# The last token tile for the first expert taken on chip, more second products held back, and the first search of the router split in two

## The chip, the cores and the metric

One core of one Trainium2 chip runs the whole program. Time is device time in microseconds (us). Five engines run side by side: TensorE (PE: products, with weight loads as PEld), VectorE (DVE), ScalarE (ACT), GpSimd (POOL) and SyncE (SP). Each works through its own instructions in order; semaphores tie them together. Sixteen DMA engines serve all queues; GpSimd starts the gathers and the accumulating copies itself, SyncE the loads of weights, ScalarE the stores of tokens.

## The reference

Three layers follow each other. The first is an attention with a decaying state. The second is a dense layer over 3072 tokens of 384 features with 2048 hidden ones. The third gives every token to one of 8 experts, each with exactly 384 places, in the order of the sorted logits:

```
x = attention(r, k, v, w, u)                 # 4 x 768 tokens -> (3072, 384)
h = x @ w_in                                 # (3072, 2048)
x = (h * sigmoid(1.702 * h)) @ w_out
logits = x @ w_gate                          # (3072, 8)
for idx in argsort(-logits.flatten()):       # greedy: token, expert = idx // 8, idx % 8
    if assigned[token] < 0 and counts[expert] < 384:
        assigned[token] = expert; counts[expert] += 1
out[mask_e] = relu(x[mask_e] @ w1[e]) @ w2[e]      # w1: 384 x 1024, w2: 1024 x 384
```

## The kernel before

Work is cut into 24 units of 128 tokens and 8 blocks of 3 units (384 tokens). Block by block the dense layer runs over 16 chunks of 128 hidden features: a first product (`Ffn.g1`, line 1207, 9 instructions: 3 feature groups by 3 pairings of high and low halves of the operands), the activation on ScalarE with the low half on VectorE, and a second product (`Ffn.g2` or single parts of it, line 1235, 9 instructions) into three accumulators, one for each tile of 128 tokens. The experts use the same class with 8 chunks each.

The program writes all instructions out by hand order. A small planner (`Issue`, object `sc`) keeps an estimated time and, for each engine, an estimated moment at which it is free. Chains of work are Python generators with a rank. They give durations to the planner, and while the loop emits PE products the planner lets chains go on whose time has come. `sc.until(...)` emits filler products until a condition holds in the plan. What the plan has put down is the order on each engine; what waits at run time is settled by semaphores.

Around the change the order is this. In the last block, the first products of all 16 chunks come first, each with a thin product for the logits (line 1479). Second products of chunks 0 and 1 (`NIN = 2`) follow at once; those of chunks 2 to 13 (`NHOLD = 12`) are held as activated tiles in a ring named `hold`, 14 and 15 in the ordinary ring. After the loop the logits of the last block are put together (lines 1569 to 1578), and the router starts.

The router (`Router.route`) works for one expert after the other. `best` finds each token's best open expert and a sort key, and ends in a first comparison table; `search` finds in five steps the threshold that fills some expert with 384 tokens. Each step is a table on VectorE, 24 small counting products on PE (line 429), and a few short operations (lines 431 to 436). Then come ranks, and `slots` (line 460) turns ranks into row numbers `idx` with a one-hot table and 24 small products (line 492). `best` for the next expert is put between these steps. Meanwhile PE does the 42 held parts (`parts_left`), tile by tile, and at the end of each tile `store_x2` copies the accumulator (line 1350) and stores it to DRAM as rows of `x2d` (line 1353). When the parts are out, `spin_wide` emits fillers (line 1783).

For expert i, `gather` (line 1671) fetches 384 rows of `x2d` by three indirect DMAs on GpSimd (line 1684), turns them round with PE transposes (line 1700), and writes a high half on ScalarE (line 1709) and a low half on VectorE (line 1711). `weights` loads eight pieces of 384 KB through the `hold` ring; `split_weights` makes a high half on ScalarE (line 1640) and a low half either on VectorE (line 1648) or by a negated copy (line 1657) and an accumulating DMA from GpSimd (line 1665). Expert 0 starts when its `ffn` is there and its first piece of weights is split:

```
sc.until(lambda: "ffn" in EX[0] and ("raw1", 0, 0) in wdone)
```

Later experts start as soon as theirs are there; until then PE may do up to two chunks of second products of the expert before.

Of the kernel before, what the change touches and what calls it, by code (L numbers as in the profile page):

```python
# [167 lines left out]
class Router:  # L168
# [7 lines left out]
    def __init__(self, nc, S, pool, bank, NJ, E, cap):  # L176
        self.nc, self.S, self.pool, self.work, self.bank, self.busy = nc, S, pool, None, bank, False
        self.NJ, self.E, self.cap = NJ, E, cap
        self.L = pool.tile([128, NJ, E], F32, name="L")

    def consts(self):
# [14 lines left out]
        nc.gpsimd.iota(jp[:, :, 1], pattern=[[0, NJ]], base=0, channel_multiplier=1,  # L196
                       allow_small_or_imprecise_dtypes=True)
# [33 lines left out]

    def t(self, name, shape, dt=F32, bufs=2):
        return self.work.tile(shape, dt, name=name, bufs=bufs)
# [7 lines left out]
    def best(self):  # L241
# [3 lines left out]
        V, L, t = self.nc.vector, self.L, self.t  # L245
        m = t("m", [128, NJ])
        V.tensor_reduce(m, L, axis=AX.X, op=OP.max)
        yield
        eq = t("eq", [128, NJ, E])
        V.tensor_tensor(eq, L, m[:, :, None].to_broadcast([128, NJ, E]), op=OP.is_equal)  # L250
        yield
        V.tensor_tensor(eq, eq, self.W[:, None, :].to_broadcast([128, NJ, E]), op=OP.mult)
        key = t("key", [128, NJ], I32)
        bits = m.bitcast(I32)
        V.tensor_scalar(key, bits, 31, -2147483648, op0=OP.arith_shift_right, op1=OP.bitwise_or)
        yield
        self.wb = t("best", [128, NJ])
        V.tensor_reduce(self.wb, eq, axis=AX.X, op=OP.max)
        V.tensor_tensor(key, key, bits, op=OP.bitwise_xor)
        yield  # L260
        self.oh = t("oh", [128, NJ, E], BF)
        V.tensor_tensor(self.oh, eq, self.wb[:, :, None].to_broadcast([128, NJ, E]), op=OP.is_equal)
        yield

        self.key = key
        h0 = t("h0", [128, NJ], I32)
        V.tensor_scalar(h0, key, 33 - HALVES[0][0].bit_length(), None, op0=OP.logical_shift_right)
        yield
        c = t("c", [128, NJ, 2], BF)
        V.tensor_copy(c, h0[:, :, None].to_broadcast([128, NJ, 2]))  # L270
        self.G0 = []
        for _ in self.compare(self.G0, c, HALVES[0][0]):
            yield
# [14 lines left out]
    def digits(self):  # L288
# [4 lines left out]
        hl = t("hl", [128, sum(ns), NJ], I32)  # L293
# [10 lines left out]
        hf = t("hf", [128, sum(ns), NJ])  # L304
# [4 lines left out]
    def route(self, out, i, found, taken):  # L309
# [4 lines left out]
        if i == 0:  # L314
            for _ in self.best():
                pass
            yield (("V", 3.4),)
# [142 lines left out]
    def slots(self, out):  # L460
# [41 lines left out]
        out["idx"] = idx  # L502
        yield (("V", 0.5),)

@with_exitstack
def kernel(ctx, tc, r, k, v, w, rk, u, us, w_in, w_out, w_gate, w1, w2, out):
# [37 lines left out]
    NIN = 2  # L544
    DLAG = 1.5
    NPE = 9
    NHOLD = 12
# [20 lines left out]
    x2d = dr.tile([NT, Dm], F32, name="x2d")  # L568
# [627 lines left out]
    class Ffn:  # L1196
# [4 lines left out]
        def g1(self, f):  # L1201
# [3 lines left out]
            for kt in range(KT):  # L1205
                for n, (a, b_) in enumerate(((0, 0), (0, 1), (1, 0))):
                    T.matmul(p, self.l1(kt, f, a), (self.xh, self.xl)[b_][:, kt],  # L1207
                             start=(kt == 0 and n == 0), stop=(kt == KT - 1 and n == 2))
                    if kt == KT - 1 and n == 2:
                        self.g1_done(f)  # L1210
                        sc.add(self.act(self, f, p, lambda: R["g1"].free(i)), 0)
                    if fine[0]:
                        sc.tensor(0.1735)
                if not fine[0]:
# [102 lines left out]
    todo = [0, 0]  # L1317

# [20 lines left out]
    def store_x2(blk, tt, acc):  # L1339
# [13 lines left out]
        nc.scalar.dma_start(x2d[j * 128:(j + 1) * 128, :], x2)  # L1353
# [119 lines left out]

    def thin_logits(f, ps):
# [54 lines left out]
    for s in range(len(seq) + 2):  # L1529
        slot[0] = s  # L1530
        fine[0] = s < begin[2]
        if s == begin[3]:
            router.consts()
            P.memset(wogp[:, NFS * 2 * E:].bitcast(F32), 0.0)
# [340 lines left out]
```

## Time and profile before

| | |
|---|---|
| three runs | 822.89, 824.23, 826.66 us (median 824.23) |
| the profiled execution | 822.38 us, its span 820.4 us |
| granted clock of TensorE | 0.998 of full speed |
| busy, of the span | PE 803.3 us (98%), PEld 756.6 (92%), DVE 622.8 (76%), ACT 472.7 (58%), POOL 140.6 (17%) |
| DMA | 105.85 MB, mean 129 GB/s |

Times in rows are counted from the first instruction. Busy time of PE includes filler products, which keep it running while it has nothing to do (lines 732 and 1783). A group's arrow shows the written tile and what it is made from. In square brackets stands the idle time of the engine just before, and what ended it.

### The profile page before, as it was taken

To read this page: it belongs to the slowest core of one execution; us is meant where nothing else is said; L and a number is where in the kernel's file an instruction comes from. 1 tells how busy PE (TensorE), PEld (TensorE's weight loads), DVE (VectorE), ACT (ScalarE), POOL (GpSimd) and SP (SyncE) were. 2 spreads that over 40 slices of the span, in tenths; PEclk is the share of its full clock that TensorE was granted. 3 is DMA by queue.
4 is the path that set the end of the run, shared out by engine and by line. 5 is a ranking of instruction groups with operands and counts; after the bars stand their busy time and mean duration, and the time that the engine had idled before them with its cause. 6 is when DMAs were issued, how large, how long until landed. Compare 5 with 4: busy or idle time off the path is not lost.

```text
span 820.4 us, 17510 instructions
## 1 busy us (share of the span) xinstructions
PE 803.3 (98%) x6608; PEld 756.6 (92%) x6608; DVE 622.8 (76%) x1424; ACT 472.7 (58%) x1178; POOL 140.6 (17%) x188
## 2 busy tenths in 40 slices
PE   8999999999999999999999999999999999999995
PEld 7898999999999999999999999988898988989995
DVE  9977898879879888888879827478888887875310
ACT  5754653575676686686676644214556645576421
POOL 1001001001201101100102000003334443454211
PEclk9999999999999999999999999999999999999999
DMA  9833634412313313303313000028889899989400
GB/s 289 227 114 107 205 117 138 130 28 84 112 32 106 112 27 98 111 23 103 111 26 107 6 12 20 2 80 223 224 222 246 240 262 244 267 226 332 89 30 29
DMA packets 46068, 105.85 MB, mean 129 GB/s; under 512 B 7352, under 2 KB 13344, under 8 KB 45984
## 3 DMA queue, kind: packets, MB, share of 16 engines
q1 hardware_dynamic: 30816, 68.21, 26.5%
q0 software_dynamic: 10416, 29.50, 16.5%
q10 hardware_dynamic: 4752, 7.03, 2.4%
q8 instruction: 51, 0.84, 0.4%
q14 instruction: 33, 0.27, 0.1%
HBM read 73.60 MB, written 10.03 MB: 102 GB/s over the span
## 4 chain that ended last, share of the span: by engine, by line
PE 84%; issue 6%; DMA 5%; DVE 2%; POOL 1%; ACT 1%; SPq 0%; POOLq 0%; ACTq 0%; DVEq 0%
PE g L1207 33%; PE acc L1235 33%; PE s L1071 3%; PE s L1153 3%; PE s L429 2%; DMA cvb<-x2d,idx 2%; PE s L809 2%; PE s L1148 1%; DMA hold<-in_w 1%; DMA nat_v<-in_v 1%; PE s L1088 1%; PE s L1103 1%; PE acc L732 1%; PE s L1479 1%; POOL out L1743 1%
## 5 line engine op out<-in xcount | busy, mean ns | idle before, releaser
L1235 PE MATMUL acc<-wk,gh 128*128 128x384 f32 x1080 | 283.2, 340 | 0.1
L1235 PEld LDWEIGHTS acc<-wk,gh 128*128 128x128 f32 x1080 | 193.3, 188 | 1.6 <-issue 0.6
L1235 PE MATMUL acc<-wk,gl 128*128 128x384 f32 x540 | 181.9, 337 | 0.0
L1207 PE MATMUL g<-xha,wk 128*128 128x384 f32 x576 | 166.1, 340 | 0.0
L1207 PE MATMUL g<-xhb,wk 128*128 128x384 f32 x576 | 164.5, 339 | 0.0
L1282 ACT ACTIVATE cvb<-cvb 128x384 f32<-128x384 f32 x240 | 122.7, 517 | 8.4 <-DVE cvb L1293 7.9
L1253 ACT ACTIVATE g<-g 128x384 f32<-128x384 f32 x128 | 60.9, 476 | 101.1 <-PE g L1207 95.9
L1207 PEld LDWEIGHTS g<-xha,wk 128*128 128x128 f32 x576 | 105.4, 188 | 1.1 <-issue 0.3
L1207 PEld LDWEIGHTS g<-xhb,wk 128*128 128x128 f32 x576 | 105.1, 188 | 0.3
L1235 PEld LDWEIGHTS acc<-wk,gl 128*128 128x128 f32 x540 | 101.4, 188 | 0.0
L1207 PE MATMUL g<-xlb,wk 128*128 128x384 f32 x288 | 97.5, 339 | 0.0
L1207 PE MATMUL g<-xla,wk 128*128 128x384 f32 x288 | 97.2, 338 | 0.0
L1056 POOL TENSOR_SCALAR_AFFINE_SELECT At<-dg 128x512 f32<-128x512 f32 x38 | 35.0, 944 | 361.1 <-DVE dg L1049 273.5
L1259 DVE TENSOR_TENSOR gl<-g,gh 128x384 fp32r<-128x384 f32 x116 | 63.5, 548 | 29.1 <-ACT gh L1256 28.9
L1266 ACT ACTIVATE gh<-g 128x384 fp32r<-128x384 f32 x64 | 31.4, 491 | 88.8 <-PE g L1207 81.5
L1269 DVE SCALAR_TENSOR_TENSOR gl<-g,gh 128x384 fp32r<-128x384 f32 x64 | 35.3, 552 | 43.7 <-ACT gh L1266 43.6
L1293 DVE TENSOR_TENSOR cvb<-cva,raw 128x768 f32<-128x768 f32 x60 | 57.2, 963 | 8.5 <-ACT cva L1350 4.8
L1256 ACT ACTIVATE gh<-g 128x384 fp32r<-128x384 f32 x116 | 56.5, 487 | 6.5 <-ACT cva L1350 2.4
L1640 ACT ACTIVATE wk<-hold 128x768 fp32r<-128x768 f32 x64 | 52.9, 840 | 10.3 <-DMA hold<-in_w 10.3
L1665 POOL DMA_DIRECT2D wk<-hold x51 | 46.4, 1026 | 65.1 <-ACT wk L1657 51.9
L1207 PEld LDWEIGHTS g<-xlb,wk 128*128 128x128 f32 x288 | 54.1, 188 | 0.1
L1207 PEld LDWEIGHTS g<-xla,wk 128*128 128x128 f32 x288 | 54.1, 188 | 0.0
(282 smaller groups left out, 1264.4 us busy)
## 6 DMA issues: line engine op xcount, KB each, us to landing
hold<-in_w SPq DMA_DIRECT2D x64, 384.0 KB, 7.7
wk<-hold POOLq DMA_DIRECT2D x51, 384.0 KB, 7.6
nat_m<-in_rk SPq DMA_DIRECT2D x15, 384.0 KB, 3.1
nat_v<-in_v SPq DMA_DIRECT2D x22, 256.0 KB, 2.9
raw<-in_w_in SPq DMA_DIRECT2D x7, 768.0 KB, 4.4
raw<-in_w_out SPq DMA_DIRECT2D x7, 768.0 KB, 4.7
nat_w<-in_w SPq DMA_DIRECT2D x22, 226.2 KB, 2.9
nat_k<-in_k SPq DMA_DIRECT2D x22, 224.0 KB, 2.6
```

Source lines behind the costliest of these rows:

```text
L1056: P.affine_select(At[s], dg[:, s::2][:, :, None].to_broadcast([128, HP, C]), pattern=[[0, HP], [1, C]], compare_op=OP.is_equal, fill=0.0, ...
L1207: T.matmul(p, self.l1(kt, f, a), (self.xh, self.xl)[b_][:, kt], start=(kt == 0 and n == 0), stop=(kt == KT - 1 and n == 2))
L1235: T.matmul(self.acc[tt], gs[a][:, tt * C:(tt + 1) * C], self.r2(f, b_), start=(f in self.cuts and n == 0), stop=(end and n == 2))
L1253: A.activation(p, p, AF.Gelu_apprx_sigmoid)
L1256: A.activation(gh, p, AF.Copy)
L1259: V.tensor_tensor(gl, p, gh.bitcast(F32), op=OP.subtract)
L1266: A.activation(gh, p, AF.Relu)
L1269: V.scalar_tensor_tensor(gl, p, 0.0, gh.bitcast(F32), op0=OP.max, op1=OP.subtract)
L1282: A.activation(t_[:, n], t_[:, n], AF.Copy, accum_out=put[n])
L1293: V.tensor_tensor(t_, x[:, None, :].to_broadcast([128, 2, Dm]), wgB[e // 4][:, (e % 4) * Dm:(e % 4 + 2) * Dm].rearrange("p (a d) -> p a d" ...
L1640: A.activation(Whi[key], raw, AF.Copy)
L1665: P.dma_start(out=Wlo[key].bitcast(F32), in_=raw, accum_op=OP.add)
```

## The change

The last block holds the second products of all chunks: `NIN = 0` and `NHOLD = 13`, so that 48 parts are left after the loop. The router's constants and `best` for all 24 columns are made in a chain `ahead` while the last block's first products run; when the last logits are there, `best` runs again for the 4 columns of the last position only (`redo`), and the plan allows 1.5 in place of 3.4 for it. The three copies of last logits become one.

`x2d` gets 128 rows of zeros at its end. For expert 0 the last tile (number 23) is numbered 24 in the row tables, so that the gathers fetch zeros for tokens of that tile and need not wait for its store. In their place, the last tile's copy in SBUF is multiplied with a one-hot matrix (an iota on GpSimd, compared on VectorE with the tile's ranks) into the accumulators, and the gathered rows are added with a product by the identity in place of a transpose. Afterwards `all_rows` computes the true row numbers, for the scatter, and restores the tables.

In `split_weights` the first piece of all takes the VectorE way, pieces 1 to 3 never do. In `best` the two chains of operations are interleaved. For expert chunk 0 the nine instructions of the first product are ordered so that those which need only high halves of x come first.

```diff
@@ Router
+        nc.gpsimd.iota(jp[:, NJ - 1, 0:1], pattern=[[0, 1]], base=NJ, ...)
+    def ahead(self):
+        for _ in self.best():
+            self.S.busy["V"] = max(self.S.t, self.S.busy["V"]) + 0.42
+            yield from self.S.room("V", 0.3)
+        self.begun = True
+        yield 0.1
@@ best(self, cols=None): on the columns `cols` of tiles kept from the first call
         V.tensor_reduce(m, L, axis=AX.X, op=OP.max)
         yield
+        V.tensor_tensor(eq, L, m..., op=OP.is_equal)
         yield
         V.tensor_scalar(key, bits, 31, -2147483648, ...)
+        V.tensor_tensor(eq, eq, self.W..., op=OP.mult)
         yield
         V.tensor_tensor(key, key, bits, op=OP.bitwise_xor)
+        V.tensor_reduce(wb, eq, axis=AX.X, op=OP.max)
         yield
+        V.tensor_scalar(h0, key, 33 - HALVES[0][0].bit_length(), None, op0=OP.logical_shift_right)
+        V.tensor_tensor(oh, eq, wb..., op=OP.is_equal)
         yield
+        V.tensor_copy(c, h0...)
         yield
+        (all columns: compare as before; else one compare of the chosen columns for each of two tables)
@@ route
-            for _ in self.best():
+            for _ in self.best(self.redo):
                 pass
-            yield (("V", 3.4),)
+            yield (("V", 1.5),)
+    def all_rows(self, out):
+        V.tensor_tensor(d, self.tt[:, 0:3], self.tt[:, 1:4], op=OP.subtract)
+        V.tensor_scalar(far, d, 128.0 * NJ - 0.5, -128.0, op0=OP.is_ge, op1=OP.mult)
+        V.tensor_tensor(out["idx"], d, far, op=OP.add)
+        V.memset(self.JP[:, NJ - 1, 0:1], NJ - 1.0)
+        V.memset(self.R[:, NJ - 1, 0, 0:1], NJ - 1.0)
@@ constants and tokens
-    NIN = 2
+    NIN = 0
-    NHOLD = 12
+    NHOLD = 13
-    x2d = dr.tile([NT, Dm], F32, name="x2d")
+    x2d = dr.tile([NT + 128, Dm], F32, name="x2d")
@@ Ffn.g1
+            steps = [(kt, n) for kt in range(KT) for n in range(3)]
+            if f == 0 and self.nf == NF3:
+                steps.sort(key=lambda x: x[1])
@@ store_x2
+        if (blk, tt) == (NBLK - 1, NU - 1):
+            kept.append((x2, sc.t, st))
+            for other in sent:
+                tc.declare_no_dep(st.ins, other.ins, ...)
+        elif (blk, tt) == (NBLK - 1, NU - 2):
+            EX[0]["x2"] = sc.t + 4.0          # before: set after the last part
@@ the last block's loop
+    def no_rows():                             # zeros to the last tile's rows and the 128 rows behind
+        P.memset(t_, 0.0)
+        for rows in (x2d[NT - 128:NT, :], x2d[NT:, :]):
+            nc.scalar.dma_start(rows, t_)
+    def ahead():                               # waits for the logits of all blocks but the last
+        router.late_consts(...); router.Gt = [...]; P.memset(...) twice
+        router.redo = slice(NC - 1, None, NC)
+        yield (("P", 1.8),)
+        yield from router.ahead()
-    sc.until(lambda: todo[0] == 0)
+    sc.until(lambda: router.begun)
@@ split_weights
-        if sc.busy["D"] > sc.t + BEHIND:
+        if m == 0 or m > 3 and sc.busy["D"] > sc.t + BEHIND:
             while sc.t < ready:
                 yield 0.1
-            if sc.busy["V"] <= sc.t + 0.2 and sc.busy["D"] > sc.t + BEHIND:
+            if m == 0:
+                yield from sc.room("V", 0.2)
+            if m == 0 or sc.busy["V"] <= sc.t + 0.2 and sc.busy["D"] > sc.t + BEHIND:
                 order[0] += 1
                 V.tensor_tensor(Wlo[key], raw, Whi[key].bitcast(F32), op=OP.subtract)
@@ gather, for i == 0
+            near = pair_[:, 1]
+            P.iota(near, pattern=[[1, NB]], base=1, ...)
+            yield from sc.room("V", 0.4)
+            V.tensor_scalar(near, near, o["rs"][:, NJ - 1:NJ], None, op0=OP.is_equal)
+            while not kept or sc.t < kept[0][1] + 0.8:
+                yield 0.1
+            first = [psum.tile([128, 512], F32, name=f"acc{a}") for a in range(NU)]
+            for a in range(NU):
+                for kt in range(KT):
+                    T.matmul(first[a][:, kt * C:(kt + 1) * C], kept[0][0][:, kt * 128:(kt + 1) * 128],
+                             near[:, a * C:(a + 1) * C], start=kt == 0, stop=False, ...)
+                yield (("T", 0.7),)
@@ land, for i == 0
+                    T.matmul(ps[:, kt * C:(kt + 1) * C], xg[a][:, kt * 128:(kt + 1) * 128], ident,
+                             start=False, stop=True, ...)
+                sc.t += 0.64
@@ gather, after the three tiles have landed
+        if i == 0:
+            router.all_rows(o)
```

## Rows read from the trace of the kernel before

**Rows 1.** Busy time by stretch: us, engines' busy time, granted clock, DMA share, GB/s.

```profile
550.24:564.30 14.06, 13.84 (x148) 10.76 (x148) 11.14 (x46) 7.30 (x12) 6.10 (x7) 1.00 0.71 184
564.30:596.64 32.34, 31.35 (x306) 28.39 (x305) 26.50 (x103) 17.80 (x28) 9.31 (x11) 1.00 0.95 252
...
665.10:699.50 34.40, 32.55 (x308) 29.66 (x308) 27.76 (x115) 18.93 (x31) 12.62 (x17) 1.00 0.99 269
```

**Rows 2.** Chain of waits near 493 us: start, us, what (one second product).

```profile
492.75 1.56 PE acc L1235 x9
```

**Rows 3.** Timeline of PE: start us, us, engine, line, operation, idle before.

```profile
529.15 0.76 PE L429 MATMUL s<-oh,cvc 128*128 128x8 bf16 x24
...
550.24 1.33 PE L1783 MATMUL g<-xhb,wogp 128*128 128x512 f32 x5
...
559.86 0.76 PE L429 MATMUL s<-oh,cvc 128*128 128x8 bf16 x24
560.85 0.52 PE L1700 MATMUL s<-ident,cvb 128*128 128x128 f32 x3 [0.23 <-DMA cvb<-x2d,idx]
...
563.38 0.76 PE L429 MATMUL s<-oh,cvc 128*128 128x8 bf16 x24
...
564.32 0.34 PE L1207 MATMUL g<-xha,wk 128*128 128x384 f32 x1
```

**Rows 4.** Timeline of VectorE, same columns.

```profile
511.96 0.56 DVE L1259 TENSOR_TENSOR hold<-g,hold 128x384 fp32r<-128x384 f32 x1 [1.38 <-ACT hold L1256]
...
525.28 0.35 DVE L247 TENSOR_REDUCE m<-L 128x24 f32<-128x192 f32 x1
...
527.12 0.17 DVE L267 TENSOR_SCALAR h<-key 128x24 int32<-128x24 int32 x1
527.32 0.19 DVE L270 CAST c<-h 128x48 bf16<-128x48 int32 x1
527.62 1.03 DVE L284 TENSOR_TENSOR cvc<-c,raw 128x768 bf16<-128x768 bf16 x2
...
552.60 0.16 DVE L501 TENSOR_TENSOR idx<-r_tt 128x3 int32<-128x3 f32 x1
...
554.79 0.44 DVE L270 CAST c<-h 128x48 bf16<-128x48 int32 x1
...
556.21 0.35 DVE L384 TENSOR_TENSOR oh<-oh,r_keep 128x192 bf16<-128x192 bf16 x1
...
563.17 0.55 DVE L1711 TENSOR_TENSOR xla<-s,xha 128x384 fp32r<-128x384 f32 x1
```

**Rows 5.** Timeline of ScalarE's queue: stores of the last two tiles.

```profile
542.63 0.33 ACTq L1353 DMA_DIRECT2D x2d<-cva  x1
...
550.96 0.33 ACTq L1353 DMA_DIRECT2D x2d<-cva  x1
```

**Rows 6.** Timeline of GpSimd: first and third of expert 0's three gathers.

```profile
554.08 1.15 POOL L1684 DMA_INDIRECT cvb<-x2d,idx  x1 [49.04 <-DVE key L255]
...
556.97 0.95 POOL L1684 DMA_INDIRECT cvb<-x2d,idx  x1 [0.30 <-issue]
```

**Rows 7.** Groups of GpSimd: count, busy us, mean ns, idle before.

```profile
L184 POOL IOTA r_d<- 128x128 f32 x1 | 0.2, 233 | 0.0
```

**Rows 8.** Timeline of PE near 132 us: 8 float products, 16 instructions.

```profile
132.54 1.16 PE L1071 MATMUL s<-nat_r,nat_k 48*128 48x128 f32 x16
```

**Rows 9.** Timelines of VectorE, then PE, at the starts of experts 3 and 4.

```profile
664.35 0.55 DVE L1711 TENSOR_TENSOR xlb<-s,xhb 128x384 fp32r<-128x384 f32 x1
...
665.12 0.42 PE L1207 MATMUL g<-xhb,wk 128*128 128x384 f32 x1
...
693.98 0.55 PE L1700 MATMUL s<-ident,cvb 128*128 128x128 f32 x3 [1.80 <-DMA cvb<-x2d,idx]
```

**Rows 10.** Timeline of VectorE near 604 us: a low half of weights.

```profile
604.22 0.96 DVE L1648 TENSOR_TENSOR wk<-hold,wk 128x768 fp32r<-128x768 f32 x1 [0.44 <-ACT wk L1640]
```

**Rows 11.** DMA issues of the page: count, KB each, us from issue to landing.

```profile
wk<-hold POOLq DMA_DIRECT2D x51, 384.0 KB, 7.6
```

More of the change, by code (lines that the diff above doesn't have):

```diff
@@ L263, in best @@
         yield
[L265 to L267 removed]
+        V.tensor_copy(c, h0[:, :, None].to_broadcast([128, n, 2]))
+        self.key, self.wb, self.oh = self.tiles[2], self.tiles[3], self.tiles[4]
         yield
[L269 to L273, printed above, removed]
+        if n == NJ:
+            self.G0 = []
+            for _ in self.compare(self.G0, self.tiles[6], HALVES[0][0]):
+                yield
+        else:
+            step, half = cols.step, NJ // len(self.Gt)
+            w = HALVES[0][0]
+            for h, g in enumerate(self.Gt):
+                at = slice(h * half + cols.start, (h + 1) * half, step)
+                k = len(range(NJ)[at])
+                V.tensor_tensor(g[:, cols.start::step, :w].rearrange("p j (a b) -> p j a b", b=2),
+                                self.pairs(self.tiles[6][:, at], w), self.numbers(k, w), op=OP.is_ge)
+                yield
@@ L1317 @@
     todo = [0, 0]
+    kept, sent = [], []
+    EX = [dict() for _ in range(E)]
     rest, stored = {}, set()
@@ L1352, in store_x2 @@
         stored.add((blk, tt))
-        nc.scalar.dma_start(x2d[j * 128:(j + 1) * 128, :], x2)
+        st = nc.scalar.dma_start(x2d[j * 128:(j + 1) * 128, :], x2)
+        if (blk, tt) == (NBLK - 1, NU - 1):
+            assert j == NJ - 1
+            kept.append((x2, sc.t, st))
+            for other in sent:
+                tc.declare_no_dep(st.ins, other.ins, reason="the first expert's gathers leave out these rows")
+        elif (blk, tt) == (NBLK - 1, NU - 2):
+            EX[0]["x2"] = sc.t + 4.0
         if blk < NBLK - 1:
@@ L1472 @@
     parts_left = [(f, tt) for tt in range(NU) for f in range(NIN, NFS)]
+    def no_rows():
+        yield from wait("cva")
+        R["cva"].free(R["cva"].new())
+        t_ = cv.tile([128, Dm], F32, name="cva", bufs=NCVA)
+        P.memset(t_, 0.0)
+        for rows in (x2d[NT - 128:NT, :], x2d[NT:, :]):
+            nc.scalar.dma_start(rows, t_)
+        yield (("P", 0.5),)
+    def ahead():
+        while todo[0] or not late:
+            yield 0.2
+        router.late_consts(cv.tile([128, 128], BF, name="raw64", bufs=2))
+        router.Gt = [cv.tile([128, NJ // 2, 128], BF, name="cvc", bufs=NCVC) for _ in range(2)]
+        for g_ in router.Gt:
+            P.memset(g_.rearrange("p a b -> p (a b)").bitcast(F32), 0.0)
+        router.redo = slice(NC - 1, None, NC)
+        yield (("P", 1.8),)
+        yield from router.ahead()
     def thin_logits(f, ps):
@@ L1585 @@
         spin()
-    EX = [dict() for _ in range(E)]
     scat = []
@@ L1683, in gather @@
             xg.append(pair_[:, a % 2])
-            P.indirect_dma_start(out=xg[a], out_offset=None, in_=x2d,
-                                 in_offset=bass.IndirectOffsetOnAxis(ap=o["idx"][:, a:a + 1], axis=0))
+            g_ = P.indirect_dma_start(out=xg[a], out_offset=None, in_=x2d,
+                                      in_offset=bass.IndirectOffsetOnAxis(ap=rows[:, a:a + 1], axis=0))
+            if i == 0:
+                for x in kept:
+                    tc.declare_no_dep(g_.ins, x[2].ins, reason="the first expert's gathers leave out these rows")
+                sent.append(g_)
             sc.busy["D"] = max(sc.busy["D"], sc.after((("P", 1.04),))) + 0.6
```

105 lines of the change are left out of this document (64 added, 41 removed).

## The prediction

> **What bounds the kernel now.** I read the clock first, then busy time by stretch, then the timelines of TensorE (PE), VectorE (DVE), ScalarE (ACT) and GpSimd (POOL) from 490 to 700 us. The granted clock is 1.00 in every stretch, and PE is busy nearly all the time [rows 1]; the clock plays no part. But busy is not useful. From 550.24 to 564.32 us PE runs the filler product of line 1783, which nobody reads, between small products of the router [rows 3]. These 14.1 us, between the last second product of the dense layer and the first product of expert 0, are the only large hole, and the change works there.
>
> What ends the hole? The router's first search starts at 525.28 and ends in the row numbers `idx`, written by 552.76 [rows 4]. The first gather starts only at 554.08 [rows 6], 1.3 us later: it reads the stored tokens, and the store of the last tile is issued at 550.96 [rows 5]; 3.1 us lie between. So two chains end there almost together, with the store last. The third gather starts at 556.97; PE is released by its landing at 560.85 [rows 3, 6]. VectorE, held up by a step of the second search, writes the low half until 563.72 [rows 4], and the first product comes at 564.32.
>
> Behind the hole the stage is not free to move. Each expert needs its own search and gather. For expert 3 the low half ends at 664.90 and PE starts at 665.12; for expert 4 PE stands 1.80 us at a gather's transposes [rows 9]. The DMA share is 0.95 in expert 0's stretch and 0.99 in expert 3's, and VectorE is busy 26.5 of 32.3 us in the first [rows 1]. PE, the searches one behind the other, and the DMA run at almost the same pace there.
>
> **The change part by part.**
>
> *Second products held.* Chunks 0 and 1 of the last block lose their second product inside the loop. One takes 1.56 us [rows 2]; two, 3.12 us. PE does them later, as 6 more of the 42 parts that cover the search. So the search starts 3.12 us earlier and PE's total is unchanged. This holds if the two shorter slots stall nowhere: VectorE must do the same logits there, and from 508 on it sits idle 1.4 us of every 1.9 [rows 4]; I take 0 (bounds 0 and 1 us).
>
> *Search partly ahead.* The first step takes 525.28 to 528.65 for 24 columns [rows 4]. It is now done earlier for all, in that idle time, and again for 4 columns: 9 small operations and 2 compares. A dependent small operation follows its predecessor by 0.20 us (527.12 to 527.32). Six dependent steps make 1.2, three partners at half that 0.3, two small compares 0.3 to 0.4: 1.9 us for 3.4, so 1.5 saved. The first counting product waited until 529.15 [rows 3], 0.5 us longer, because the written plan put it there; the plan's allowance falls from 3.4 to 1.5, so it moves 1.9. I take 1.9 (bounds 1.4 and 2.2). With the 3.12 that is 5.0: `idx` at 547.75 instead of 552.76.
>
> *The gathers.* They leave out the last tile (zero rows stand in for it), so they wait for the store of the last but one, issued in the trace at 542.63 [rows 5]. With 3.12 earlier and 4 more parts of 0.52 before it, and its place among search steps, it stays near 541 to 542 and lands by 545. `idx` is last: gathers start near 547.9 instead of 554.08, 6.2 us earlier, and the third lands at 554.5 instead of 560.7.
>
> *The product from the chip.* One GpSimd iota of 384 columns (128 columns took 233 ns; I take 0.5, bounds 0.23 and 0.7 [rows 7]) stands in its queue behind the three gathers, so it ends near 552.3; one VectorE compare, 0.3; then 9 exact products of 128 columns. Such float products come as two instructions; 8 took 1.16 us [rows 8], so 9 take 1.3. The last tile's copy is ready near 551.4, since PE's parts now end near 550.9 (550.24, less 3.12, plus 3.12, plus 0.6 for the 24 small products of the slots, as long as a counting step of rows 3, that now fall before). So these end near 554.2, when the gather lands. The 9 products that replace 9 transposes cost 1.3 instead of 1.0 and lie mostly under the landing. The last three, ScalarE's copy of 0.5 and the plan's steps follow: expert 0 starts near 557.0 (bounds 555.6 by data alone, 558.5 with a VectorE collision as now). That is 7.3 us earlier. New order of the first chunk's products saves up to 0.5 inside these bounds.
>
> *First weights.* Their load follows the search, 5.0 us earlier; the second chunk's is no longer held to the end of the parts. The first low half is a VectorE subtract, 0.96 us [rows 10], instead of an accumulating DMA, which lands 7.6 us after issue [rows 11]. It arrives in time, but later splits wait in order behind it. Its queue place is where VectorE is planned free, which I put after the masking at 556.21 less 5.0 [rows 4]. The DMA stream as a whole starts 5 to 7 us earlier.
>
> *What is late next.* The second search. It moves 5.0 with `idx`, not 7.3, and gets new work on VectorE. The compare for the one-hot waits for an iota queued behind gathers that end 4.0 us after `idx` (554.08 to 557.92 for the three [rows 6], and 0.15 ahead), so 4.5 with the iota; the second search's instructions stand behind that wait. Placed after the masking (3.8 us behind `idx`), it costs 0.7 and the compare 0.3. The subtract costs 0.96, less a hole of 0.6 us while PE counts: 0.4. Restoring the row numbers, 5 small operations, costs 0.4. The second search now meets expert 0's first products 2 us sooner: 0.3. Sum 2.1. Interleaving the two halves of `best` hides a dependent step and a planned one, about 0.3 per search: 0.3 for expert 1, 1.2 by expert 4. So x of expert 1 comes 3.2 us earlier, of expert 4 4.1. Bounds: 0 if the wait stands right behind `idx` (4 us), 6 if all new work falls into holes.
>
> While PE is 7.3 early and x 3 to 4, second products fill for 1.56 each; by expert 3 both are used up already in the trace of before (PE starts it within 0.3 us of its x [rows 9]), so PE gets what the search gets: 4.1 us. From expert 5 on nothing more is lost. Sum: 7.3 less 3.2 given back = 4.1.
>
> On a lock: beside the first gather a cast of VectorE took 0.44 us, and ended with the gather, where the same cast took 0.19 in the first search [rows 4, 6]. The Trainium skill ("SBUF — State Buffer", Who interferes with whom) says that a cast or tensor_scalar in a two-port mode and a GpSimd instruction block each other for the whole instruction. By that rule all three gathers, now beside more of these operations, could each hold one for up to 1.1 us; by the row it is 0.25 once.
>
> **The rivals.**
>
> *PE keeps it all* (7.3 us): if the searches are not the limit behind the hole. For it: PE idles only 0.99 us in expert 0's stretch and 1.85 in expert 3's [rows 1]. Against: [rows 9]. Time 824.2 - 7.3 = 816.9.
>
> *The wait stands early, or gathers hold VectorE.* The one-hot's compare right behind `idx` makes VectorE wait 4.2 us instead of 0.7; or three holds of 1.1. The second search then moves 5.0 - 2.1 - 3.5, the interleaving gives back 1.2: 0.6 us, 823.6. For it: the queue is in order, and the row of 0.44 us. Against: the router's own steps are planned back to back there and take the place first. The lock rule above is one form of this.
>
> *The gathers still wait for the last store.* Parts end 0.6 later, so the first gather starts at 554.7 and nothing is gained: 824.8. Against: the dependence is declared away in both directions.
>
> *Slower: the first subtract finds no place.* All later splits of weights wait in order behind it. Its plan wants VectorE free within 0.2 us. If it slips three counting steps (3.5 us each, as 559.86 to 563.38 [rows 3]), it runs near 563, the next split's accumulate is issued near 566 and lands near 573, against a need at about 561: PE stands some 11.6 us after two first products, 4.3 more than the 7.3 won: 828.5. It decides from two slips on. For it: VectorE's load [rows 1]. Against: each counting step leaves a hole.
>
> **How the numbers follow.** The profiled execution took 822.38 us (span 820.4 and 2.0 around it); the median of the three runs is 824.23. 822.4 - 4.1 = 818.3 against the first, 820.1 against the median; I give 820.0. Chances: forecast 0.43 (own range 817.5 to 821.8, half of it below 820.1), PE keeps it all 0.22, early wait or lock 0.19, gathers still wait 0.07, slower 0.09. Half a per cent, 4.1 us, is about what a measurement of this kernel can tell from no change. Faster by more: 0.22 + 0.27 = 0.49; slower by more 0.09; between 0.42. The range reaches from 815.5 (all kept, by the data bound of 555.6) to 825.0, leaving out the slower case.
>
> **What would show it.** Right: the first masking step of the search about 5 us earlier; the first gather within 0.3 us of `idx` instead of 1.3; expert 0's first product near 557; fillers of line 1783 falling from 14 to about 6 us; and then the lead shrinking from 7 to about 4 by expert 3, with more fillers or standing ahead of experts 1 to 3. Wrong: a lead that stays at 7 through expert 4 (searches not the limit), a VectorE wait of 3 us right behind `idx`, a first gather later than 552, or a first split of weights after 558.

## The result: slower by 1.1%

The changed kernel takes 834.15 us (832.80 to 834.87, 4 runs), the kernel before 824.61 us beside it (822.89 to 826.66, 4 runs): ratio 1.0113, 95% interval 1.0086 to 1.0140. I forecast 820.0 and gave slower by more than half a per cent a chance of 0.09. The profiled execution took 834.09 us (span 832.4), so 12.0 us more span than before.

The same stretches after (us, engines' busy time, granted clock, DMA share, GB/s), against [rows 1]:

```profile
550.24:562.60 12.36, 11.26 (x112) 9.84 (x112) 8.12 (x31) 7.37 (x11) 5.03 (x8) 1.00 0.79 215
562.60:595.52 32.92, 32.77 (x333) 30.07 (x331) 27.70 (x107) 14.71 (x25) 9.16 (x12) 1.00 0.67 157
595.52:634.54 39.02, 34.64 (x328) 31.89 (x324) 28.95 (x105) 24.18 (x39) 15.99 (x23) 0.96 0.92 251
634.54:676.63 42.09, 39.10 (x411) 35.95 (x408) 34.04 (x134) 18.64 (x30) 14.82 (x18) 0.92 0.74 187
```

The hole before expert 0 shrank from 14.1 to 12.4 us. Experts 0 to 4 start at 562.60, 595.52, 634.54, 676.63 and 707.10 us; before, at 564.32, 596.64, 629.64, 665.12 and 699.53. So the change leads by 1.7 and 1.1 us, then lies 4.9, 11.5 and 7.6 us behind. Experts 5 to 7 start 8.4, 11.9 and 12.2 us behind. Most of the loss is made in the stretches of experts 1 and 2 (39.0 and 42.1 us, before 33.0 and 35.5). There PE stands or spins, and the granted clock, 1.00 in each of these stretches before, falls to 0.96 and 0.92. In the worst place it is 1.00 up to 669.5 us and 0.50, the lower of the two levels, from 670 to 676, after PE had been busy 0.95 of the 2.00 us from 666 to 668.

The router explains why so little of the lead is there. Its chain of waits after (start, us, what), where before the landing of a gather stood on it (3.75 us at 556.97):

```profile
548.42 0.16 DVE idx L523
...
549.64 0.74 POOL cvb L1752
...
551.11 1.11 POOL cvb L1752
...
552.53 0.95 POOL cvb L1752
...
553.48 0.47 POOL cvb L1768
...
553.99 0.43 DVE cvb L1771
...
554.56 0.91 PE acc L1779 x6
...
557.89 2.01 PE acc L1793 x18
559.90 0.58 PE s L451 x24
...
562.76 1.07 PE g L1245 x6
```

The gathers are on it by GpSimd's order, not by their data: behind them stands the iota, behind that VectorE's compare, then PE's products. The second search lies on VectorE in between (start, us, operation, idle before):

```profile
551.77 0.35 DVE L406 TENSOR_TENSOR oh<-oh,r_keep 128x192 bf16<-128x192 bf16 x1
553.99 0.42 DVE L1771 TENSOR_SCALAR cvb<-cvb,rs 128x384 f32<-128x384 f32 x1 [1.87 <-POOL hold L1685]
554.32 0.95 DVE L1715 TENSOR_TENSOR wk<-hold,wk 128x768 fp32r<-128x768 f32 x1
...
556.19 0.15 DVE L453 TENSOR_SCALAR ge<-s 64x8 bf16<-64x8 f32 x1
...
560.52 0.16 DVE L453 TENSOR_SCALAR ge<-s 64x8 bf16<-64x8 f32 x1 [1.80 <-PE s L451]
560.60 1.47 DVE L1807 TENSOR_TENSOR xla<-acc,xha 128x384 fp32r<-128x384 f32 x3
```

It stands 1.87 us for GpSimd, spends 0.42 on the compare and 0.95 on the first subtract, and later 1.80 us waiting for its counting products, which PE runs only behind the 18 products with the identity (2.17 us from 557.73). From ranks to ranks the second search takes 34.7 us, before 29.1. The first ranks come 4.2 us earlier than before (543.57 against 547.78), the second ones 1.35 us later (578.26 against 576.91). So the second search alone eats the lead of the first search.

Searches 3 to 5 together then take 99.6 us, before 91.3. Two things are seen in them. VectorE's subtracts of low halves between 550 and 700 us (count, busy us, mean ns, idle before), before and after:

```profile
L1648 DVE TENSOR_TENSOR wk<-hold,wk 128x768 fp32r<-128x768 f32 x3 | 2.9, 953 | 0.4 <-ACT wk L1640 0.4
```

```profile
L1715 DVE TENSOR_TENSOR wk<-hold,wk 128x768 fp32r<-128x768 f32 x9 | 8.6, 954 | 0.6 <-ACT wk L1705 0.6
```

And PE's waits from 564 to 700 us for the search's comparison `ge` (us, times, longest), of which the kernel before has none:

```profile
PE s L456 <- DVE ge L453: 6.5, 6, 1.5
```

Both meet in this piece of the fourth search (VectorE):

```profile
624.67 0.16 DVE L453 TENSOR_SCALAR ge<-s 64x8 bf16<-64x8 f32 x1 [1.46 <-PE acc L1272]
624.78 0.96 DVE L1715 TENSOR_TENSOR wk<-hold,wk 128x768 fp32r<-128x768 f32 x1
625.65 0.16 DVE L458 TENSOR_REDUCE nm<-s 128x1 f32<-128x8 f32 x1
...
628.06 0.15 DVE L453 TENSOR_SCALAR ge<-s 64x8 bf16<-64x8 f32 x1
628.14 0.94 DVE L1715 TENSOR_TENSOR wk<-hold,wk 128x768 fp32r<-128x768 f32 x1
629.00 0.15 DVE L458 TENSOR_REDUCE nm<-s 128x1 f32<-128x8 f32 x1
```

`nm` (line 458) needs `ge` and one small product of PE. Each subtract, written between the two, holds it for 0.9 us. And `ge` itself starts at 624.67, although the 24 counting products end at 623.36. PE had reached the next product of the search and stood:

```profile
622.60 0.76 PE L451 MATMUL s<-oh,cvc 128*128 128x8 bf16 x24
623.22 0.42 PE L1272 MATMUL acc<-wk,gl 128*128 128x384 f32 x1
623.48 0.52 PE L1272 MATMUL acc<-wk,gh 128*128 128x384 f32 x2
624.88 0.16 PE L456 MATMUL s<-ge,r_ones 64*128 64x8 bf16 x1 [0.89 <-DVE ge L453]
```

I call a `ge` that starts over 0.9 us behind its counting products, with VectorE idle that long, a late release. The profiled execution has 6 between 545 and 745 us, 9.3 us in all; that of the kernel before has none. In all 6 GpSimd works at an indirect DMA, a gather or a scatter of rows, when the counting products end; here it is the third gather of an expert:

```profile
622.96 0.95 POOL L1752 DMA_INDIRECT cvb<-x2d,idx  x1 [0.30 <-issue]
```

### The profile page after: what moved, and what is told of

Read it like the earlier page. It is cut to its first block, busy times and chain, and to the rows that moved or that the text cites. A ratio compares the mean times of both kernels' runs of the same rounds, so it can differ in the third digit from the quotient of the medians.

```text
span 832.4 us, 17610 instructions
## 1 busy us (share of the span) xinstructions
PE 807.3 (97%) x6659; PEld 762.0 (92%) x6659; DVE 629.1 (76%) x1446; ACT 468.0 (56%) x1172; POOL 135.0 (16%) x185
## 4 chain that ended last, share of the span: by engine, by line
PE 86%; issue 5%; DMA 3%; DVE 2%; POOL 1%; ACT 1%; POOLq 0%; ACTq 0%; another core or an unknown queue 0%; DVEq 0%
PE g L1245 33%; PE acc L1272 32%; PE s L1106 3%; PE s L1188 3%; PE s L451 2%; PE acc L767 2%; DMA cvb<-x2d,idx 2%; PE s L844 2%; PE s L1183 1%; PE s L1123 1%; DMA wk<-hold 1%; PE s L1138 1%; PE s L1789 1%; PE s L1545 1%; POOL out L1841 1%
## 5 line engine op out<-in xcount | busy, mean ns | idle before, releaser
L1290 ACT ACTIVATE g<-g 128x384 f32<-128x384 f32 x128 | 61.0, 476 | 98.7 <-PE g L1245 91.3
L1732 POOL DMA_DIRECT2D wk<-hold x45 | 41.2, 1012 | 92.4 <-ACT wk L1724 80.8
```

What stands on the lines that cost most here:

```text
L1290: A.activation(p, p, AF.Gelu_apprx_sigmoid)
L1732: P.dma_start(out=Wlo[key].bitcast(F32), in_=raw, accum_op=OP.add)
```

## The experiments

The kernels ran in five batches, each on one chip (batches 3 and 5 on the same one), with runs of the kernel before beside them. The table gives for each: the ratio to the kernel before; the pieces of weights (8 for each expert, from 0) whose low half VectorE subtracts, as far as piece 41; the stretch from the last dense block's first product to the end of the span; the second search, from ranks to ranks; searches 3 to 5; late releases. The stretch is used because profiled executions differ by about 2.1 us ahead of block 1 (it starts near 88.7 or near 91.0 us), whatever the kernel: in the six late ones, and in no other, the granted clock is 0.50 from 57.1 to 59.8 us, with PE busy all the time. A stretch comes from one profiled execution, the ratio from all runs.

| batch, kernel | ratio (95%) | pieces on VectorE | stretch | 2nd | 3rd-5th | late |
|---|---|---|---|---|---|---|
| before | 1 | 13 15 19 | 336.0 | 29.1 | 91.3 | 0 |
| changed | 1.0113 (1.0086-1.0140) | 0 7 13 16 19 21 27 35 38 | 348.0 | 34.7 | 99.6 | 6 |
| 1 plain_gather | 1.0158 (1.0125-1.0192) | 0 4 12 18 20 30 37 | 352.7 | 31.9 | 98.1 | 6 |
| 1 old_split | 1.0030 (1.0010-1.0049) | 13 14 27 30 | 340.9 | 34.3 | 93.7 | 4 |
| 1 no_ahead | 1.0093 (1.0059-1.0127) | 0 5 15 16 19 21 | 351.9 | 37.6 | 98.8 | 4 |
| 1 held_alone | 1.0121 (1.0084-1.0159) | 4 8 15 17 20 | 351.0 | 31.7 | 98.3 | 7 |
| 2 after_few_sub | 1.0127 (1.0103-1.0151) | 0 41 | 345.4 | 33.9 | 96.0 | 0 |
| 2 held_few_sub | 1.0092 (1.0063-1.0121) | none | 343.3 | 29.3 | 94.5 | 0 |
| 2 before_sub47 | 1.0085 (1.0059-1.0112) | 4 7 10 14 16 21 | 342.4 | 29.6 | 96.4 | 0 |
| 2 before_land | 1.0027 (1.0013-1.0041) | 13 15 19 | 336.9 | 29.1 | 91.7 | 0 |
| 3 after_nin2 | 1.0117 (1.0067-1.0167) | 0 5 15 16 19 21 | 348.6 | 36.5 | 95.2 | 4 |
| 3 nin2_old_split | 1.0137 (1.0088-1.0185) | 2 7 13 16 19 21 27 35 38 | 351.5 | 36.6 | 98.0 | 5 |
| 3 held_ring12 | 1.0170 (1.0120-1.0220) | 4 8 15 17 20 | 354.8 | 31.8 | 100.0 | 7 |
| 3 before_ring13 | 1.0000 (0.9980-1.0021) | 13 15 19 | 339.7 | 29.4 | 92.3 | 4 |
| 4 after_set | 1.0042 (1.0026-1.0058) | 13 15 19 | 338.7 | 34.5 | 90.3 | 0 |
| 4 held_set | 0.9996 (0.9984-1.0009) | 13 15 19 | 337.0 | 29.3 | 93.4 | 0 |
| 4 after_near | 1.0047 (1.0029-1.0064) | as changed | 340.3 | 36.1 | 91.5 | 0 |
| 4 old_split_near | 1.0023 (1.0006-1.0039) | as old_split | 339.0 | 37.7 | 90.4 | 0 |
| 5 after_set_near | 1.0083 (1.0061-1.0106) | 13 15 19 | 338.9 | 35.9 | 89.8 | 0 |
| 5 set_near_split | 1.0046 (1.0027-1.0064) | 13 15 19 | 340.3 | 35.0 | 92.1 | 0 |

Late releases go by the batch: every profile of batches 1 and 3 has 4 to 7, none of batches 2, 4 and 5 has one. They do not go by the chip, since batches 3 and 5 had the same. The medians of the kernel before go the same way: 824.6 us beside the changed kernel, 824.8 and 826.5 in batches 1 and 3, but 821.8, 822.5 and 821.5 in the others. Where they fall goes by the written order: `held_alone` and `held_ring12`, in different batches, turn out to have the same instructions in the same order on every engine, and have 7 each at the same steps of the search. One of them, in `held_alone` and then in `held_ring12`:

```profile
641.60 0.17 DVE L431 TENSOR_SCALAR ge<-s 128x8 bf16<-128x8 f32 x1 [2.45 <-PE acc L1235]
```

```profile
641.53 0.17 DVE L431 TENSOR_SCALAR ge<-s 128x8 bf16<-128x8 f32 x1 [2.52 <-PE acc L1235]
```

And the steps are those beside GpSimd's indirect DMAs. In each of the 47 late releases an indirect DMA is at work between the counting products and `ge`. Count the steps at which VectorE had finished within 0.3 us of the counting products: in the nine profiles with late releases 43 of the 68 with an indirect DMA in the 0.9 us behind the products are late, and none of the 169 without one; in the other eleven profiles there are 85 with one, and none is late. So the indirect DMA is a condition but not enough. What sets the batches apart is not known, and GpSimd's times in a profile are rough.

So ratios are compared inside a batch first.

**Batch 1: one part at a time.** Theory A: the product from the chip holds the second search. Theory B: VectorE's subtracts do. Theory C: the held products do. The letters come back in the expectations below.

`plain_gather`: all rows gathered after the last store, no zero rows, no one-hot.

```diff
-            EX[0]["x2"] = sc.t + 4.0      # after the last tile but one
+            EX[0]["x2"] = sc.t + 4.0      # after the last tile
-        if i == 0: near = ..., products with the one-hot, identity products, all_rows
```

> Leaves out of the change the product from the chip: expert 0's 384 rows are all gathered once the last store is in, and turned round by transposes; the held parts, the search partly ahead, the rule for first weights and the interleaved best stay. Theory A (the product from the chip, in order on TensorE and VectorE, holds the second search back by 5.5 us, and the later searches and their rows grow from that): the second search takes about 29 us again, not 34.7, expert 0 starts 563 to 566, expert 3 near 664 instead of 676.6, and the time is 820 to 825, as before or a little below. Rival B (the new rule for the first weights moves low halves to VectorE later on and loads the searches there): 832 to 836, as the changed kernel. Rival C (held parts and interleaved best make the plan run ahead of what happens): 830 or more too.

Expert 0 starts 85.8 us after the last dense block, before 79.9. The second search comes back to 31.9 us, as A says, but the time is the worst of the batch. The product from the chip alone is not what makes the whole slow.

`old_split`:

```diff
-        if m == 0 or m > 3 and sc.busy["D"] > sc.t + BEHIND:
+        if sc.busy["D"] > sc.t + BEHIND:
```

> The changed kernel with the rule of before for which low halves of weights VectorE subtracts (no exception for pieces 0 to 3). Theory A: the second search is as slow as in the changed kernel (34 us), time 830 to 836. Rival B: number of VectorE subtracts back from 19 to about 13, experts 2 and 3 start within 2 us of the kernel before, time 822 to 826.

Most of the loss is gone, with the second search as long as in the changed kernel (34.3) and 4 late releases (6.5 us). A can hold for some 0.3% here, and B looks right so far.

`no_ahead`: `best` for all 24 columns after the last logits; the chain `ahead` is gone.

```diff
-            for _ in self.best(self.redo):
+            for _ in self.best():
-            yield (("V", 1.5),)
+            yield (("V", 3.4),)
```

> The changed kernel with the whole first best done after the last logits, as before (allowance 3.4 instead of 1.5 in the plan). Theory A: idx about 1.5 to 2 us later than 548.4, the second search still 34 us, time 833 to 838. Rival C, if the plan's lead comes from the first search: 824 to 828.

The first ranks come 2.0 us later after the last block's start than in the changed kernel (61.3 against 59.3 us); the ratio is no higher. A start 2 us earlier is worth nothing that these runs can tell.

`held_alone`, in the kernel before (to make room, three small tiles of the router have one buffer each; so too in the other `held` kernels and in `before_ring13`):

```diff
-    NIN = 2
-    NHOLD = 12
+    NIN = 0
+    NHOLD = 13
...
-            if f2 < NIN:
-                last.g2(f2)
```

> The kernel before with the second products of all 16 chunks held (NIN 0, NHOLD 13) and nothing else of the change. Theory A: the first search starts 2.3 us earlier, the parts end 1 us later, the first gather waits for the last store as before: 823 to 826, no change. Rival C (held parts are what costs): 829 or more.

The largest surprise: this edit alone costs as much as the whole change. Its written order puts pieces 4 and 8 on VectorE, which before subtracts none below 13.

**Batch 2: fewer, more, or a mere shift.** Theory D came up: any new written order costs. `after_few_sub`, `held_few_sub`:

```diff
-        ... sc.busy["D"] > sc.t + BEHIND:
+        ... i > 4 and sc.busy["D"] > sc.t + BEHIND:
```

> The changed kernel in which VectorE subtracts the low half only of the first piece of all and of pieces from expert 5 on (so none of the 9 subtracts that run between 555 and 700 us there). Theory B in its wide form (each low half on VectorE, 0.96 us, stands in the queue of the search and lengthens it; before has 3 of them between 550 and 700 us, the changed kernel 9): the six searches from the first ranks to the seventh take 177 to 184 us instead of 193, time 823 to 828. Theory D (the order written by the plan is sensitive as a whole, and before sits at a good point of it: any shift costs some us whatever is shifted): anything from 826 to 838, not tied to the number of subtracts.

> The kernel before with all second products held (836.3) and VectorE subtracts only from expert 5 on. Theory B: 824 to 829, the searches back to 177 to 184 us. Theory D: within 4 us of 836 or anywhere above 828.

Wide B falls: without the subtracts it isn't fast again. The low halves then go by accumulating DMA, and PE waits for one in `held_few_sub`, in the middle of the fourth search (expert 2 starts at 635.7 us there, before at 629.6):

```profile
621.58 0.62 PE L1207 MATMUL g<-xhb,wk 128*128 128x384 f32 x2 [2.02 <-DMA wk<-hold]
```

`before_sub47`, in the kernel before:

```diff
-        if sc.busy["D"] > sc.t + BEHIND:
+        if m in (4, 7) or sc.busy["D"] > sc.t + BEHIND:
```

> The kernel before, in which the low halves of pieces 4 and 7 are put on VectorE (as the kernel with all second products held does by itself, at 575 and 583 us), nothing else. Theory B: 1 to 2 us later from the second search on for each, 826 to 830. Theory D: a larger or an arbitrary change, 830 or more.

0.85%, in a batch without late releases, against 0.27% for the mere shift beside it. The forced pieces moved the plan's own choice too (10, 14, 16, 21 in place of 13, 15, 19), so this is the price of a whole written order and not of two subtracts. One way in which they cost is that of 628.14 us above, here in the second search, which is 0.5 us longer than before (29.6 against 29.1):

```profile
573.19 0.17 DVE L431 TENSOR_SCALAR ge<-s 128x8 bf16<-128x8 f32 x1 [0.27 <-PE s L429]
573.28 0.95 DVE L1650 TENSOR_TENSOR wk<-hold,wk 128x768 fp32r<-128x768 f32 x1
574.15 0.16 DVE L436 TENSOR_REDUCE nm<-s 128x1 f32<-128x8 f32 x1
```

`before_land`:

```diff
-    LAND = 3.4
+    LAND = 3.5
```

> The kernel before with the plan's allowance for the landing of a gather at 3.5 instead of 3.4 us (experts 1 to 7), a change of the written order alone. Theory B: within 1.5 us of before, 823 to 826. Theory D: 827 or more, since a shift that means nothing costs as much as the change does.

0.27%, 2.2 us: one shift that means nothing costs some 2 us. That no other costs more is not shown.

**Batch 3: do parts add up?** Theory E says that they do, and that holding the last two products is what costs. `after_nin2` has `NIN = 2`, `NHOLD = 12`; `nin2_old_split` the old rule too; `held_ring12` lets the weights use 12 of the 13 buffers (`R["hold"].ok(2)`); `before_ring13` has only `NHOLD = 13`.

> The changed kernel with second products held as before (two done in the loop, NIN 2, NHOLD 12); the product from the chip, the search partly ahead and the new rule for first weights stay. Counted from the last block's first product to the end of the profiled span, holding all second products alone cost 15 us (351.0 against 336.0), the whole change 12.0, the product from the chip gave back 4.7 and the search ahead 3.9. Theory E (holding the last two products is what costs, and the parts add up): about 333 us for that stretch, time 820 to 824. Theory B (the subtracts of the new rule cost by themselves): 826 to 831. Theory D (only the plan's luck): no sum of parts holds, 828 or more.

> The same with the old rule for first weights too, so that of the change the product from the chip, the search ahead and the interleaved best remain. Theory E with parts that add up: 12.0 less 15 less 7.1 is 10 us below before, 813 to 818. Theory A (the product from the chip holds the second search): 824 to 828. Theory D: 826 or more.

> All second products held and nothing else of the change, but the weights of the experts use at most 12 of the 13 buffers, as before. If the thirteenth buffer costs (weights loaded one piece earlier, so that the plan puts low halves on VectorE between 575 and 625 us): 824 to 829. If it is the later end of the parts and the later first gather that cost: 833 to 838.

> The kernel before with 13 buffers in the ring that the experts' weights use, and no other change. If the thirteenth buffer costs: 829 to 836. If not: 823 to 826.

E falls: forecasts of 813 to 824, measured 1.012 and 1.014. The old rule now chose 2, 7, 13, 16, 19, 21, 27, 35, 38: nearly the pieces of the changed kernel. So the rule as such does not settle which pieces are picked. `held_ring12` tests nothing: its limit never took hold, it is the program of `held_alone` once more, at 1.0170 in place of 1.0121 (the intervals overlap). That the thirteenth buffer costs nothing is shown by `before_ring13` alone. It has nearly the written order of before (some ten of PE's 6,608 products stand elsewhere), yet 4 late releases (7.0 us) and a stretch 3.7 us longer, at a ratio of 1.000: in that batch the kernel before seems to pay for them too.

**Batch 4: the same pieces, or no wait for GpSimd.** `after_set` and `held_set` force pieces 13, 15 and 19; `after_near` and `old_split_near` replace the iota:

```diff
+        if m in (13, 15, 19) or i > 4 and sc.busy["D"] > sc.t + BEHIND:
```

```diff
-            P.iota(near, ...)
-            V.tensor_scalar(near, near, o["rs"][:, NJ - 1:NJ], None, op0=OP.is_equal)
+            for a in range(NU):
+                V.tensor_scalar(near[:, a * C:(a + 1) * C], router.io, a * 128.0 + 1.0, o["rs"][:, NJ - 1:NJ],
+                                op0=OP.add, op1=OP.is_equal)
```

> The changed kernel in which, before piece 45, VectorE subtracts the low halves of pieces 13, 15 and 19 and no others: the very ones it subtracts in the kernel before (the changed kernel: 0, 7, 13, 16, 19, 21, 27, 35, 38, 44). Theory B in its narrow form (low halves put on VectorE among the first pieces, or too few of them behind, lengthen searches 3 to 5, which take 99.6 us instead of 91.3): those three searches within 2.5 us of 91.3, time ratio 1.000 to 1.005. Theory D (luck of the written order): ratio 1.008 to 1.016, whatever the pieces.

> The kernel before with all second products held (ratio 1.012) and the same three pieces, 13, 15 and 19, on VectorE before piece 43, instead of 4, 8, 15, 17 and 20. Theory B, narrow: ratio 0.998 to 1.004. Theory D, or a cost of the held products as such: 1.008 to 1.015.

> The changed kernel in which the one-hot for the product from the chip is compared with the router's own table of 0 to 127, in three compares of 128 columns, so that VectorE no longer waits for GpSimd's numbers behind the gathers (1.87 us). Theory A: the second search falls from 34.7 by 1.5 to 2 us, TensorE's wait of 1.07 before the products goes, expert 0 starts 1 us earlier, ratio 1.008 to 1.011; of a gain in the second search the later ones keep what they don't lose to their own waits. Rival: VectorE is held at the next wait instead, for the landing (1.80 us idle, at TensorE's counting products): no change, 1.010 to 1.014.

> The same compare in the kernel with the old rule for first weights (ratio 1.003): if both causes add, the ratio falls by 0.002 to 0.003, to 1.000 to 1.001, and the second search from 34.3 to about 32.5; if the searches behind take the gain back, 1.002 to 1.005.

`held_set` is the kernel before in time: in this batch and with these pieces, holding all second products costs nothing, and gains nothing. `after_set` has the same held products and the same early pieces, and on top the search ahead, the product from the chip and the rest: 0.46% more (1.0042 less 0.9996). Inside that batch this is the price of the change's core.

`after_near` has the written order of the changed kernel, but for the iota and the compare. The wait is gone:

```profile
551.81 0.67 DVE L1770 TENSOR_SCALAR cvb<-raw,rs 128x128 f32<-128x128 bf16 x3
552.40 0.95 DVE L1715 TENSOR_TENSOR wk<-hold,wk 128x768 fp32r<-128x768 f32 x1
```

Expert 0 leads by 3.0 us, counted from the last block (76.9 against 79.9), but the second search takes 36.1 us: it gains 1.3 us at its second step and loses them beside expert 0's first products. And the same step of the fourth search, which in the changed kernel was released 1.31 us late, is on time, 0.04 us behind its counting products, although the third gather lies beside it as there (PE, VectorE, GpSimd):

```profile
621.92 0.76 PE L451 MATMUL s<-oh,cvc 128*128 128x8 bf16 x24
```

```profile
622.72 0.16 DVE L453 TENSOR_SCALAR ge<-s 64x8 bf16<-64x8 f32 x1
```

```profile
622.34 0.95 POOL L1752 DMA_INDIRECT cvb<-x2d,idx  x1 [0.30 <-issue]
```

Searches 3 to 5 take 91.5 us, 8 less than in the changed kernel, with all its pieces on VectorE. `after_set`, with other pieces, comes to the same ratio. So in this batch neither the pieces nor the wait separate the two. What both have and the changed kernel's profile has not is a batch without late releases; that these make most of the difference from 1.0113 is argued, not shown.

**Batch 5: both mends**, and the identity products of the three tiles written 0.75 apart (`xt = [max(x, sc.t + 0.75 * a) ...]`).

> Both mends in the changed kernel: pieces 13, 15 and 19 on VectorE as before (alone 1.0042), and the one-hot compared with the router's table, without the wait for GpSimd (alone 1.0047). The changed kernel lies at 1.011, so either alone takes 0.7 of it; if the two losses were apart, the sum is below zero: 0.997 to 0.999. If both act by the same path (the run falls behind the written order in searches 2 to 4, and either mend ends that), little is left to gain: 1.001 to 1.004. The second search stays at 33 to 36 us, since TensorE still has the 18 products with the identity ahead of the counting step.

> The same with the products by the identity written 0.75 us apart for the three tiles, so that the second search's threshold product stands after the first tile's six and not after all 18. If TensorE's order holds the second search: 1.4 us less in it than in the run beside it, and a ratio lower by 0.001 to 0.002. If the second search is not what paces the experts behind any more: the same ratio within 0.002.

They don't add: 1.0083, in the written order of `after_set` (1.0042) less one wait. Two batches differ that much, 0.4%, with nothing in the profiles to show why; the profile of `after_set_near` is of the fastest of its six runs (824.98 us, median 828.25), so it need not hold the loss. The split order makes 0.9 us of the expected 1.4 in the second search (35.0 against 35.9); the ratio falls by 0.0037, more than expected (the intervals still touch), and pieces 42, 46 and 48 moved with it, so the two aren't told apart. No version clearly beats the kernel before.

## Why the prediction was wrong

**Start of the search: nearly right.** Forecast 5.0 us earlier, measured 4.2 (`idx` at 548.42). Two second products gave 2.0 (`held_alone`, 523.30 against 525.28) to 2.3 us (here, 522.98) of 3.1, and the first counting product moved from 529.15 to 524.93 [rows 3].

**The gathers: a row misread.** I took the 1.3 us between `idx` and the first gather for the last store [rows 4 to 6]. With the store out of the way 1.06 remain (548.58 to 549.64), and expert 1 had 0.8 in the trace of before (582.06 to 582.84). So 1.7 us of the forecast 6.2 were not there.

**The product from the chip: mis-sized.** Nine exact products were 1.3 us from [rows 8], whose products have 48 rows. With 128 rows, 18 instructions take 2.17 us, the products with the one-hot are another 18, and the compare ahead of them waited 1.87 us where I had 0.7. Expert 0 starts at 562.60, not 557.0.

**What is late next: the step that failed.** I let the second search lose 2.1 us and gain 0.3, so that expert 1's rows come 3.2 us earlier (bounds 0 and 6). Its `idx` comes 1.7 later (583.58 against 581.90). The search loses 5.6. The rows have 1.87 us of wait, 0.42 compare, 0.95 subtract and 1.80 for PE's order in it, the rest beside expert 0; these are not prices that come back one by one, since without the first wait (`after_near`) it takes 36.1 us. I had followed VectorE's queue, but not that the identity products stand on PE ahead of the next counting step. All 11 kernels with the product from the chip have 33.9 to 37.7 us there, all 9 others 29.1 to 31.9: that the product from the chip lengthens this search is shown, in every batch that has kernels of both kinds. Leaving it out gives back 2.8 of the 5.6 (`plain_gather`, 31.9). With 5.6 in place of 2.1 the forecast gain of 4.1 would have been 0.6, a forecast of no change.

For searches 3 to 5 I had put no loss and a gain of 0.3 each. They take 8.3 us longer, more than the second search does: this term, put at a gain, is the larger part of the miss, and what follows is about it.

**First weights: priced once.** I put 0.4 us for one subtract. But the plan chooses VectorE wherever it holds the DMA for late, and with loads 5 us earlier it chose other pieces, 9 subtracts up to 700 us for 3. That a subtract written between `ge` and `nm` holds the search for 0.9 us is shown in the rows. What early pieces cost in all is not: in the kernel before they came with another written order (0.85%), and in the changed kernel they could not be separated.

**"From expert 5 on nothing more is lost"** fell too: the loss is 7.6 us at expert 4 and 12.2 at expert 7. The 8.3 us of searches 3 to 5 stand beside five of the six late releases, 8.1 us, in the same execution. Nearly the same program without them (`after_near`) is at 1.0047. So my reading: some 0.4% is the change, and the rest up to 1.13% comes where `ge` is released late, at steps that the written order puts beside a gather or a scatter. Against it speak `old_split`, at 1.003 with 4 late releases, and `after_few_sub` and `after_set_near`, at 1.0127 and 1.0083 with none. The changed kernel itself was not run again beside `after_near`, so the cause of this part stays open.

**The rivals.** The slower one had its first subtract near 563; it ran at 554.32, and PE never stood for the first weights. "PE keeps it all" and "gathers wait" fell as well. The early wait was the nearest: the compare stands behind the masking, where the forecast had it, but with too small a price. The chances had a slip: half of 0.43 is 0.22, not the 0.27 that went into "faster by more". On the lock: beside the gathers one cast took 0.32 us (550.47) against 0.19 [rows 4], and it ended with the gather. The Trainium skill ("SBUF — State Buffer", Who interferes with whom) says that a cast in a two-port mode and an instruction of GpSimd's keep each other out, the first one for its whole length; from that I had up to 1.1 us for each gather, and no operation of VectorE's there is longer by that much. The other way round, a gather of `after_near` takes 1.87 us (552.30), the two before it 1.16 and 1.13, with VectorE's compare and its subtract of 0.95 beside it; so GpSimd is the one that looks held. Whether the late `ge`, which wait beside gathers as well, are of that kind is not shown: they are up to 2.7 us late, and in batches 2, 4 and 5 there are none.

## What to carry to other kernels

Before pricing an earlier start, ask which chain paces the next stage, here one search behind the other on VectorE, and count everything that the new work puts into its queues on both sides of each handover. When an order is written by a planner, list which choices change with the shift (here which low halves go to which engine), not only the part that was edited. To compare versions at half a per cent, run the changed kernel itself in the same batch as its mends; the same chip is not enough, as batches 3 and 5 show (the kernel before took 826.5 and 821.5 us there).

## What I had not expected of the hardware

VectorE's comparison started 1.0 to 2.7 us behind the last counting product in 4 to 7 of 35 steps, in all profiles of some batches and in none of others, each time with an indirect DMA of GpSimd at work in between. VectorE was idle over most of that time, and the profile names a later product, or another source ("remote"), as what released it. The Trainium skill ("Perfetto Trace Analysis", Tensor Engine Instruction) says that a matmul's end in the profile is estimated from its size, so the products or the signal may have been late; no run here tells which, nor why it happens only beside indirect DMAs and only in some batches.
